# Accumulating transfers for two row-sum folds a batch, and the last half folded like the others

## The chip, the cores and the metric

One core of a Trainium2 chip runs the whole program. The metric is device time in microseconds (us); the kernel before takes 1115.96 us (median of three runs, 1114.64 to 1117.03).

## The reference

Pooled attention over 8 batches and 8 heads, followed by a top-1 mixture of experts. Shapes: q, k, v are 8 x 8 x 1152 x 64.

```python
q_pool = q.reshape(B, H, S // 2, 2, D).mean(axis=3)          # 576 queries
scores = scale * np.matmul(q_pool, k.transpose(0, 1, 3, 2))
attn = np.exp(scores - max(scores)); attn /= sum(attn) + 1e-09
x = np.matmul(attn, v)                                       # -> 4608 tokens of 512
logits = x @ w_gate; expert = argmax(logits); gate = softmax(logits)[expert]
out = gate * (np.maximum(x @ w1[expert], 0) @ w2[expert])
```

## The kernel before, in words

The attention comes first, the experts behind it. The attention is cut into 64 units: batch b (8), head pair hp (4 a batch), half (288 of the 576 queries). A unit is written here as (hp, half) of its batch. In a unit `scores` makes nine score products on TensorE (L640, each four matmuls on 64x64 quarters of the array, from 1,152 keys in nine chunks of 128), VectorE copies each one out of PSUM and takes its minimum (L644), the minima are spread over the partitions by a small product (L665), and ScalarE takes the exponentials in place, two chunks an instruction (L675). The tile `s` holds them: 128 partitions x 9 chunks x 2 heads x 288. `values` multiplies the exponentials by v (L779).

The softmax's divisor, the sum over 1,152 keys, is made in `chunk_sum`. It is the part that changes:

- Most units are folded on POOL into a tile `fold` of three chunks, by three adds: chunks 0 to 2 plus 3 to 5 (`fold<-s`), plus chunks 6 to 8 (`fold<-fold,s`, both 128 x 1728), and the third of the three onto the first (`fold<-fold`, 128 x 576). When both halves of a pair are folded, TensorE adds over the partitions with matmuls by a matrix of ones on 32-column tiles (`total`, L725): two groups of four.
- The last half of a batch, (3,1), has only the first add on POOL (L731); TensorE takes the other six chunks' worth itself (`whole`, L718): three groups of four beside the one of `total` for the other half of the pair.
- The last pair of the last batch is summed by TensorE alone.

There are three `fold` buffers and four `s` buffers. A fold buffer comes free when the pair's sum on TensorE has read it. POOL also adds neighbouring queries (`qp<-qn`, L529), issues six scatters a batch that enter the tokens into the experts' lists (L960), and later the experts' gathers. The loads of q, k and v are issued by SP.

The order of the work is written by a planner (`Flow.emit`, L135): every step has an engine, an assumed duration, a key (its rank), what it depends on and the buffers it holds; each engine takes the ready step with the lowest key, and the resulting order is then fixed for each engine. The constants `R_...` and `K_...` are added to the keys. TensorE's steps also carry the tiling they use (`COLS` for 32-column tiles, `QUADS` for quarters), and the planner prefers to stay in one.

Of the kernel before, what the change touches and what calls it, by code (L numbers as in the profile page):

```python
# [32 lines left out]
K_POOL = -28  # L33
# [4 lines left out]
K_SUM = 25  # L38
K_AV = 42
K_FREE = -25  # L40
R_Q = 18
R_K = 14
R_SCORE = -2
R_TAKE = -12
R_BIAS = -29
R_FOLD3 = 22
R_VALUE = 4
R_ADD = -17
R_LOGIT = -3
K_ROW = 33  # L50
K_ROUTE = 59
# [221 lines left out]
def kernel(  # L273
# [210 lines left out]
    def load_pair(o, f, key, b, hp):  # L484

        x = Pools()
        x.later, x.late = {}, hp
        opening = not o.exact and b == 0 and hp == 0
        if opening:
            return first_pair(o, f, key, x)  # L490

        kp = tile_of(o, "kp", [P, NQD * NC, BL], bufs=2, pool=o.ld)
        qn = tile_of(o, "qn", [P, NJ, NB, 2, BL], pool=o.ld)
        x.vn = vn = tile_of(o, "vn", [P, 2, NC, D], bufs=3, pool=o.rt)
        qp = tile_of(o, "qp", [P, NJ, NB, BL], pool=o.ld)
        x.kT = kT = tile_of(o, "kT", [P, NC * P], bufs=KT_BUFS, pool=o.kq)
        x.qT = qT = tile_of(o, "qT", [P, NQ], bufs=KT_BUFS, pool=o.kq)

        load = lambda out, src: nc.sync.dma_start(out=out, in_=src)
        rows = NQD * NC  # L500

        def quarters(t, src, n0=0, n1=rows):

            for h in range(2):
                for i in range(D // BL):
                    g = (h * D // BL + i) * BL
                    load(t[g:g + BL, n0:n1], src[h][:, i * BL:(i + 1) * BL].rearrange("(p n) d -> p n d", p=BL)[:, n0:n1])

        def k_part(n0, n1, ns, move, after=()):
            return f.carry("SP", ns, lambda: quarters(kp.t, heads(k, b, hp), n0, n1), key + K_LOAD, after, [kp], move)  # L510

        start = not o.exact and b == 0 and hp == 1

        def q_part(n0, n1, ns, move):
            return f.carry("SP", ns, lambda: quarters(qn.t.rearrange("p j b t d -> p (j b t) d"), heads(q, b, hp), n0, n1),
                    key + K_LOAD, (), [qn], move, 3000 if first and hp == 2 else 0)

        js = [slice(half * NJ // 2, (half + 1) * NJ // 2) for half in range(2)]
        first = not o.exact and b == 0
        paced = first and hp < 3  # L520
        move = 2600 if o.exact else 4400
        k0 = k_part(0, rows, 1900, move, done(not start and o.asked or None))
        cuts = [(0, rows // 2), (rows // 2, rows)] if start else [(0, rows)]
        q0 = [q_part(n0, n1, 1900 // len(cuts), move // len(cuts)) for n0, n1 in cuts]
        vb = heads(v, b, hp).rearrange("h (p b c) d -> b p h (c d)", b=NQD, c=NC)
        x.v = f.carry("SP", 1900, lambda: [load(vn.t[i * BL:(i + 1) * BL].rearrange("p h c d -> p h (c d)"), vb[i]) for i in range(NQD)],
                      key + K_V, done(q0[-1] and q0[-1][9][0]), [vn], 2600 if o.exact else 2200)
        parts = js if start else [slice(0, NJ)]
        q1 = [f.add("POOL", pool(NJ * QP // len(parts)), lambda j=j: nc.gpsimd.tensor_tensor(  # L529
            qp.t[:, j], qn.t[:, j, :, 0, :], qn.t[:, j, :, 1, :], ALU.add), key + K_POOL, done(got), [qn, qp])  # L530
            for j, got in zip(parts, q0)]
        q1 = [q1[0], q1[-1]]
        o.asked = q0[-1] and q0[-1][9][0]
        key += K_PIECE + (START if start else 0)
        x.k, x.q = {}, {}

        def turn_k(c0, n):
            nc.vector.transpose(kT.t.rearrange("p (c b i) -> p b c i", b=NQD, i=BL)[:, :, c0:c0 + n],
                                kp.t.rearrange("p (b c) d -> p b c d", b=NQD)[:, :, c0:c0 + n])

        def turn_q(half):
            nc.vector.transpose(qT.t.rearrange("p (j b i) -> p j b i", b=NB, i=BL)[:, js[half]], qp.t[:, js[half]])

        def turned(half):
            x.q[half] = done(f.add("DVE", turn_ns(HQ), lambda: turn_q(half), key + 7 * half + R_Q, done(q1[half], paced and o.pace or None), [qT, qp]))
            o.turned.extend(x.q[half])

        turned(0)
        for c0 in range(0, NC, TURN):
            n = min(TURN, NC - c0)  # L550
            e = f.add("DVE", turn_ns(n * P), lambda c0=c0, n=n: turn_k(c0, n), key + 2 + c0 / 2 + R_K, done(k0, paced and o.pace or None), [kT, kp])
            o.turned.extend(done(e))
            x.k.update((c, done(e)) for c in range(c0, c0 + n))
        turned(1)
        return x

# [64 lines left out]
    def scores(o, f, key, x, half, step=None):  # L621
# [8 lines left out]
        for c in range(NC):  # L630
            if half == 0 and c in x.later:
                x.later[c](done(m))
            pt = score_banks(o)

            def product(c=c, pt=pt):

                for i in range(2):
                    for h in range(2):
                        up, to = slice(h * D, (h + 1) * D), slice(i * D, (i + 1) * D)
                        nc.tensor.matmul(pt.t[to, h, :HQ], x.kT.t[up, c * P + i * D:c * P + (i + 1) * D], x.qT.t[up, cols],  # L640
                                         start=True, stop=True, tile_position=(up.start, to.start))

            def take(c=c, pt=pt):
                nc.vector.tensor_scalar(  # L644
                    s.t[:, c], pt.t[:, :, :HQ], -SCALE, None, op0=ALU.mult, op1=ALU.min, accum_out=mx.t[:, c:c + 1],
                )

            at = key + 20.0 * c / NC
            m = f.add("PE", 485, product, at + R_SCORE, done(*x.q[half], *x.k.get(c, ())), [pt, s, x.kT, x.qT], QUADS)
            o.turned.extend(done(m))  # L650
            if half == 1 and c == 3 - x.late:
                o.pace = m
            taken.append(f.add("DVE", dve(2 * HQ), take, at + R_TAKE, done(m), [pt, s]))
        if o.exact:
            for h in range(2):
                rowwise(o, s.t[:, :, h])
# [4 lines left out]
        def spread():  # L661
            for i in range(2):
                for j in range(2):
# [3 lines left out]

        m = f.add("DVE", 150, lambda: nc.vector.tensor_reduce(top.t, mx.t, axis=AX.X, op=ALU.min),
                  key + 20 + K_MAX, done(*taken))
        m = f.add("PE", 130, spread, key + 20 + K_TOP, done(m), [pb], QUADS)  # L670
        m = f.add("DVE", 290, lambda: nc.vector.tensor_reduce(bias.t, pb.t[:, :, :D], axis=AX.XY, op=ALU.min),  # L671
                  key + 20 + K_TOP + R_BIAS, done(m), [pb])

        def expo(c0, n):
            nc.scalar.activation(s.t[:, c0:c0 + n], s.t[:, c0:c0 + n], AF.Exp, bias=bias.t, scale=-1.0)  # L675
# [2 lines left out]
        for c0 in range(0, NC, step or NC):  # L678
            n = min(step or NC, NC - c0)
            e = f.add("ACT", act(2 * n * HQ) + 190, lambda c0=c0, n=n: expo(c0, n),  # L680
                      key + 20 + K_EXP + c0, done(m), [s])
            made += [e] * n
        return s, made

# [20 lines left out]
    def chunk_sum(o, f, key, s, ready, b, hp, half, sm, last):  # L705
# [1 line left out]

        key += K_SUM
        by_units = not o.exact and b == B - 1 and hp >= NHP - LAST
        on_pe = by_units or not o.exact and hp == NHP - 1 and half == 1  # L710
        if half == 0 or by_units:
            o.pair, ps = None, None

        def whole(ps, begin, chunks):
            for i, chunk in enumerate(chunks):
                for h in range(2):
                    to = slice(64 * (i % 2) + 32 * h, 64 * (i % 2) + 32 * h + 32)
                    nc.tensor.matmul(ps.t[to, 0, :HQ], ones4[:, hp, half, :], chunk[:, h], start=begin and i < 2,  # L718
                                     stop=i + 2 >= len(chunks), tile_position=(0, to.start))

        def total(ps, u, half, begin):
            for i in range(2):
# [10 lines left out]
        elif not on_pe:  # L733
            u = tile_of(o, "fold", [P, 3, 2, HQ], bufs=FOLD_BUFS, pool=o.rt)
            add = lambda to, a, b: nc.gpsimd.tensor_tensor(to, a, b, ALU.add)  # L735
            p = f.add("POOL", pool(6 * HQ), lambda: add(u.t, s.t[:, 0:3], s.t[:, 3:6]), key, every(ready[:6]), [s, u])
            p = f.add("POOL", pool(6 * HQ), lambda: add(u.t, u.t, s.t[:, 6:9]), key, done(p, *every(ready[6:])), [s, u])
            p = f.add("POOL", pool(2 * HQ), lambda: add(u.t[:, 0], u.t[:, 0], u.t[:, 2]), key + R_FOLD3, done(p), [u])
            if half == 0:
                o.pair = (u, p)  # L740
                u.left += 1
# [3 lines left out]
        if o.pair:  # L745
            v, q = o.pair
            v.left -= 1
            parts.append(lambda: total(ps, v, 0, True))
            needs, holds, ns = done(q), [ps, v], 485
        begin = not parts  # L750
        if half_way:
            parts.append(lambda: whole(ps, begin, [*(u.t[:, c] for c in range(3)), *(s.t[:, c] for c in range(6, NC))]))
# [4 lines left out]
        else:  # L757
            parts.append(lambda: total(ps, u, 1, begin))
            needs, holds, ns = [*needs, *done(p)], [*holds, u], ns + 485
        p = f.add("PE", ns, lambda: [part() for part in parts], key + 15 - 5 * on_pe, needs, holds, COLS)  # L760
        if not last:
            return [f.add("ACT", act(HQ) - 44, lambda: nc.scalar.copy(sm.t, ps.t[:, 0, :HQ]), key + 15, done(p), [ps, sm])]
        return [f.add("DVE", dve(HQ), lambda: nc.vector.tensor_tensor(sm.t, sm.t, ps.t[:, 0, :HQ], ALU.add),
# [2 lines left out]
    def values(o, f, key, x, s, ready, hp, half, xT):  # L766
# [4 lines left out]
        for c in range(NC):  # L771
# [7 lines left out]
                        mark.made = nc.tensor.matmul(pa.t[cs, i, :HQ], x.vn.t[up, h, c, :], s.t[up, c, h],  # L779
                                                     start=c == 0, stop=c == NC - 1, tile_position=(up.start, cs.start))  # L780

            p = f.add("PE", 485, product, key + 20.0 * c / NC + R_VALUE, done(p, x.v, ready[c]), [pa, x.vn, s], QUADS)
            mark.step = p
            o.marks.append(mark)
        a = f.add("ACT", act(HQ) - 44, lambda: nc.scalar.copy(xT.t[:, hp, to], pa.t[:, 0, :HQ]), key + 20 + K_FREE, done(p), [pa, xT])
# [25 lines left out]
        return f.add("DVE", 600, inverse, key, done(p), [ps, rec])  # L811

    def attend(o, f, key, b, hp, xT, sm, summed):
        x = load_pair(o, f, key, b, hp)
        outs = []
        end = not o.exact and hp == NHP - 1 and b == B - 1
# [9 lines left out]
    def routing(o, f, key, b, xT, rec, ready, hold=()):  # L826
# [15 lines left out]

        if b is not None:
            f.add("DVE", 150, lambda: nc.vector.tensor_reduce(flg[:, b:b + 1], recf(), axis=AX.XY, op=ALU.max),
                  at, ready, [rec])
        pl = pt = pr = value_banks(o) if b == B - 1 else score_banks(o)

        aside = lambda at, n: pt.t[:QP, 1, at:at + n]
# [711 lines left out]
```

## Time and profile before

| | us |
|---|---|
| median of 3 runs | 1115.96 |
| profiled execution, its own time | 1113.62 |
| its span, first to last instruction | 1111.7 |
| TensorE (PE) busy in the span | 1100.8 |
| POOL busy in the span | 854.2 |
| granted TensorE clock, mean share | 0.999 |

The attention takes about the first 650 us, the experts the rest. One batch of the attention repeats every 80.07 us. PE, PEld, DVE, ACT, POOL and SP are TensorE's matmuls, its weight loads, VectorE, ScalarE, GpSimd and SyncE. An fp32 matmul stands in the trace as two records, so a group of four matmuls is eight records.

### The profile page before, as it was taken

The numbers are of one execution on the slowest core, as the hardware profiler recorded it, in microseconds if no ns is written. First come the engines' busy times: TensorE is split into PE (matmuls) and PEld (weight loads), VectorE is DVE, ScalarE is ACT, GpSimd is POOL, SyncE is SP. The second block draws the span as 40 slices with busy tenths as digits, with TensorE's granted clock in tenths as the row PEclk, the third lists the DMA queues.
The fourth block names the chain that finished last, engine by engine and source line by source line (L and its number), as shares of the span: only waits on it lengthen the run. The fifth ranks groups of instructions, "written<-read, shape, count | busy, mean of one in ns | idle before, by whom it ended". The sixth has DMA issues, their size and how long they took to land.

```text
span 1111.7 us, 32995 instructions
## 1 busy us (share of the span) xinstructions
PE 1100.8 (99%) x13317; PEld 793.8 (71%) x13317; DVE 875.5 (79%) x2244; ACT 624.2 (56%) x835; POOL 854.2 (77%) x488
## 2 busy tenths in 40 slices
PE   9999999999999999999999999999999999999997
PEld 5555556565655565665665568999888989899896
DVE  7988988989989989989999959755555556677761
ACT  4656666566565666557655564444444444555561
POOL 3999999999999999999999943766666655555511
PEclk9999999999999999999999999999999999999999
DMA  9976747738648558558545069865555566677640
GB/s 159 167 120 111 128 76 123 129 66 125 115 73 139 97 85 141 94 89 146 81 84 107 3 227 212 244 180 176 176 169 167 184 195 191 194 248 252 224 159 30
DMA packets 387502, 158.06 MB, mean 142 GB/s; under 512 B 302694, under 2 KB 357762, under 8 KB 387342
## 3 DMA queue, kind: packets, MB, share of 16 engines
q1 hardware_dynamic: 376718, 134.91, 55.7%
q0 software_dynamic: 10464, 20.78, 5.8%
q8 instruction: 106, 1.74, 0.7%
q14 instruction: 54, 0.44, 0.2%
q10 hardware_dynamic: 160, 0.20, 0.1%
HBM read 135.02 MB, written 22.07 MB: 141 GB/s over the span
## 4 chain that ended last, share of the span: by engine, by line
PE 87%; issue 7%; POOL 4%; DVE 1%; DMA 1%; POOLq 0%; ACT 0%
PE st L640 24%; PE pa L779 24%; PE ph L1363 16%; PE py L1393 16%; PE st L725 3%; POOL fold L735 2%; PE st L718 1%; DVE s L644 1%; POOL xr L1092 1%; PE st L856 1%; PE st L665 1%; POOL out_dram L1402 1%; POOL xq L1092 1%; PE st L801 0%; DMA xr<-x_runs,ix 0%
## 5 line engine op out<-in xcount | busy, mean ns | idle before, releaser
L675 ACT ACTIVATE s<-s,bias 128x1152 f32<-128x1152 f32 (+1 forms) x320 | 346.7, 1149 | 172.5 <-DVE bias L671 172.4
L644 DVE TENSOR_SCALAR_CACHE_REDUCE s<-st 128x576 f32<-128x576 f32 x576 | 416.1, 746 | 30.3 <-PE st L640 28.1
L640 PE MATMUL st<-qT,kT 64*64 64x288 f32 x4608 | 363.6, 406 | 1.5 <-DVE s L644 0.9
L779 PE MATMUL pa<-s,vn 64*64 64x288 f32 x4608 | 358.5, 403 | 0.3 <-DVE xT L786 0.3
L640 PEld LDWEIGHTS st<-qT,kT 64*64 64x64 f32 x4608 | 167.4, 133 | 115.3 <-DVE s L644 22.4
L779 PEld LDWEIGHTS pa<-s,vn 64*64 64x64 f32 x4608 | 172.2, 133 | 98.4 <-DVE xT L786 3.5
L735 POOL TENSOR_TENSOR fold<-s 128x1728 f32<-128x1728 f32 x55 | 212.9, 3870 | 4.6 <-ACT s L675 4.4
L735 POOL TENSOR_TENSOR fold<-fold,s 128x1728 f32<-128x1728 f32 x55 | 213.4, 3879 | 0.5
L1363 PE MATMUL ph<-xh,w1h 128*128 128x248 f32 (+4 forms) x512 | 155.8, 304 | 0.6 <-DVE hl L1373 0.6
L1363 PE MATMUL ph<-xl,w1h 128*128 128x248 f32 (+4 forms) x512 | 154.6, 302 | 0.0
L1363 PE MATMUL ph<-xh,w1l 128*128 128x248 f32 (+4 forms) x512 | 154.6, 302 | 0.0
L1235 DVE TENSOR_TENSOR w2l<-raw,w2h 128x1024 fp32r<-128x1024 f32 x64 | 78.3, 1223 | 85.0 <-ACT w2h L1320 81.3
L1092 POOL DMA_INDIRECT xr<-x_runs,ix x76 | 96.8, 1274 | 51.8 <-issue 23.9
L1393 PE MATMUL py<-w2h,hh 128*128 128x512 f32 x328 | 128.1, 391 | 0.0
L1393 PE MATMUL py<-w2l,hh 128*128 128x512 f32 x328 | 127.8, 390 | 0.0
L1393 PE MATMUL py<-w2h,hl 128*128 128x512 f32 x328 | 127.8, 390 | 0.0
L1402 POOL DMA_INDIRECT out_dram<-y,rec x41 | 44.0, 1073 | 90.0 <-ACT y L1410 73.1
L1371 ACT ACTIVATE hh<-ph 128x372 fp32r<-128x372 f32 (+4 forms) x100 | 49.3, 493 | 106.5 <-PE ph L1363 106.4
L1363 PEld LDWEIGHTS ph<-xh,w1h 128*128 128x128 f32 x512 | 96.4, 188 | 3.4 <-DVE hl L1373 1.5
L1363 PEld LDWEIGHTS ph<-xl,w1h 128*128 128x128 f32 x512 | 96.5, 188 | 0.8
L1363 PEld LDWEIGHTS ph<-xh,w1l 128*128 128x128 f32 x512 | 96.5, 188 | 0.0
L1373 DVE SCALAR_TENSOR_TENSOR hl<-ph,hh 128x372 fp32r<-128x372 f32 (+4 forms) x100 | 55.6, 556 | 48.6 <-ACT hh L1371 48.5
(230 smaller groups left out, 1339.0 us busy)
## 6 DMA issues: line engine op xcount, KB each, us to landing
raw<-in_moe_w_dram SPq DMA_DIRECT2D x128, 512.0 KB
kp<-in_k_dram SPq DMA_DIRECT2D x124, 144.0 KB
vn<-in_v_dram SPq DMA_DIRECT2D x124, 144.0 KB
qn<-in_q_dram SPq DMA_DIRECT2D x120, 144.0 KB
x_runs<-row SPq DMA_DIRECT2D x96, 99.0 KB
xr<-x_runs,ix POOLq DMA_INDIRECT x76, 4.7
x_runs<-empty SPq DMA_DIRECT2D x4, 297.0 KB
xq<-x_runs,ix POOLq DMA_INDIRECT x52, 2.9
```

The lines of the kernel that those rows point to most:

```text
L640: nc.tensor.matmul(pt.t[to, h, :HQ], x.kT.t[up, c * P + i * D:c * P + (i + 1) * D], x.qT.t[up, cols], start=True, stop=True, tile_position ...
L644: nc.vector.tensor_scalar(s.t[:, c], pt.t[:, :, :HQ], -SCALE, None, op0=ALU.mult, op1=ALU.min, accum_out=mx.t[:, c:c + 1],)
L675: nc.scalar.activation(s.t[:, c0:c0 + n], s.t[:, c0:c0 + n], AF.Exp, bias=bias.t, scale=-1.0)
L735: add = lambda to, a, b: nc.gpsimd.tensor_tensor(to, a, b, ALU.add)
L779: mark.made = nc.tensor.matmul(pa.t[cs, i, :HQ], x.vn.t[up, h, c, :], s.t[up, c, h], start=c == 0, stop=c == NC - 1, tile_position=(up.sta ...
L1092: ins = nc.gpsimd.indirect_dma_start(out=x.xr[i // NQD].t[:, i % NQD, :], out_offset=None, in_=xg, in_offset=bass.IndirectOffsetOnAxis(ap= ...
L1235: (nc.gpsimd if eng == "POOL" else nc.vector).tensor_tensor(lo, raw, hi.bitcast(F32), ALU.subtract)
L1363: mark.made = nc.tensor.matmul(view()[:, i, :], a[:, c, fp], b[:, c, :n], start=c == 0 and k == 0, stop=c == NDC - 1 and k == 2)
L1371: a = f.add("ACT", act(nb * n) - 44, lambda home=home, apart=apart: nc.scalar.activation(home(0), apart(), AF.Relu), at - 20, done(p), [ph ...
L1373: d = f.add("DVE", dve(nb * n), lambda home=home, apart=apart: nc.vector.scalar_tensor_tensor(home(1), apart(), 0.0, home(0).bitcast(F32), ...
L1393: mark.made = nc.tensor.matmul(py.t, blocks(a)[:, c * x.nr + r], b[:, c % 2, :], start=c == 0 and k == 0, stop=c == NFC - 1 and k == 2)
L1402: ins = nc.gpsimd.indirect_dma_start(out=out, out_offset=bass.IndirectOffsetOnAxis(ap=x.re.t.bitcast(I32)[:, r, 0:1], axis=0), in_=y.t, in ...
```

## The change

From the second batch on (b > 0, `o.later`), the steps get ranks of their own: each `R_...` constant becomes a pair, the second of which is for later batches, and five new ones are added (the short list below shows three). For b = 1 to 6 the second add of units (0,0) and (2,0) is no longer a POOL add but a transfer that POOL issues and that adds chunks 6 to 8 into the fold tile (`dma_start` with `accum_op`). And only in batch 0 does the last half still go to TensorE (`on_pe`); in batches 1 to 6 it is folded by three POOL adds like any other. The variable `one` is always false, so what hangs on it does nothing.

```diff
-R_Q = 18
-R_FOLD3 = 22
+R_Q = 18, 37
+R_FOLD3 = 22, 40
+R_SUM = 0, -1
+R_EXP = 0, 38
+R_POOL = 0, -21
...
-        on_pe = by_units or not o.exact and hp == NHP - 1 and half == 1
+        on_pe = by_units or not o.exact and b == 0 and hp == NHP - 1 and half == 1
...
+        one = not o.exact and (False)
...
-            p = f.add("POOL", pool(6 * HQ), lambda: add(u.t, u.t, s.t[:, 6:9]), key, done(p, *every(ready[6:])), [s, u])
-            p = f.add("POOL", pool(2 * HQ), lambda: add(u.t[:, 0], u.t[:, 0], u.t[:, 2]), key + R_FOLD3, done(p), [u])
+            if not o.exact and (half == 0 and 0 < b < B - 1 and hp % 2 == 0):
+                p = f.add("POOL", 1100, lambda: nc.gpsimd.dma_start(out=u.t, in_=s.t[:, 6:9], accum_op=ALU.add), key, done(p, *every(ready[6:])), [s, u])
+                p = f.add("DMA", 4700, lambda: None, key, done(p), [s, u], late=800)
+            else:
+                p = f.add("POOL", pool(6 * HQ), lambda: add(u.t, u.t, s.t[:, 6:9]), key, done(p, *every(ready[6:])), [s, u])
+            p = f.add("POOL", pool(2 * HQ), lambda: add(u.t[:, 0], u.t[:, 0], u.t[:, 2]), key + R_FOLD3[o.later], done(p), [u])
...
-        p = f.add("PE", ns, lambda: [part() for part in parts], key + 15 - 5 * on_pe, needs, holds, COLS)
+        p = f.add("PE", ns, lambda: [part() for part in parts], key + 15 - 5 * on_pe + R_SUM[o.later], needs, holds, COLS)
...
     def attend(o, f, key, b, hp, xT, sm, summed):
+        o.later = int(not o.exact and b > 0)
```

On TensorE before, around the sum of the fourth batch's last pair (`fold_4723` is unit (3,0), `fold_4858` unit (3,1), `pa` and `st` the products with v and the scores):

```order
L640 MATMUL st_5040<-qT_4870,kT_4721 64x288 x4
L779 MATMUL pa_4947<-s_4568,vn_4222 64x288 x4
L725 MATMUL st_5057<-fold_4723,ones_73 32x288 x4
L718 MATMUL st_5057<-fold_4858,ones_73 32x288 x6
L718 MATMUL st_5057<-s_4568,ones_73 32x288 x6
L640 MATMUL st_5083<-qT_4870,kT_4721 64x288 x4
```

The same place on TensorE in the changed kernel (`fold_4710` is (3,0), `fold_4837` is (3,1)):

```order
L645 MATMUL st_5047<-qT_4718,kT_4731 64x288 x4
L645 MATMUL st_5052<-qT_4718,kT_4731 64x288 x4
L732 MATMUL st_5060<-fold_4710,ones_73 32x288 x4
L732 MATMUL st_5060<-fold_4837,ones_73 32x288 x4
L645 MATMUL st_5079<-qT_4718,kT_4731 64x288 x4
```

Sixteen matmuls of the sum have become eight, and the sum now needs the finished fold of (3,1). On POOL before, from the same batch's last half to the next batch's first units (`fold_4932` is the next batch's (0,0), `fold_5089` its (0,1)):

```order
L735 TENSOR_TENSOR fold_4723<-fold_4723,s_4433 128x1728
L529 TENSOR_TENSOR qp_4840<-qn_4331 128x576
L731 TENSOR_TENSOR fold_4858<-s_4568 128x1728
L735 TENSOR_TENSOR fold_4723<-fold_4723 128x576
L735 TENSOR_TENSOR fold_4932<-s_4690 128x1728
L529 TENSOR_TENSOR qp_4990<-qn_4860 128x576
L735 TENSOR_TENSOR fold_4932<-fold_4932,s_4690 128x1728
L735 TENSOR_TENSOR fold_4932<-fold_4932 128x576
L735 TENSOR_TENSOR fold_5089<-s_4814 128x1728
```

And on POOL in the changed kernel (`fold_4976` is the next batch's (0,0), `fold_5087` its (0,1)):

```order
L742 TENSOR_TENSOR fold_4837<-s_4558 128x1728
L534 TENSOR_TENSOR qp_4882<-qn_4569 128x576
L742 TENSOR_TENSOR fold_4837<-fold_4837,s_4558 128x1728
L742 TENSOR_TENSOR fold_4710<-fold_4710 128x576
L742 TENSOR_TENSOR fold_4976<-s_4685 128x1728
L742 TENSOR_TENSOR fold_4837<-fold_4837 128x576
L745 DMA fold_4976<-s_4685 128x1728
L534 TENSOR_TENSOR qp_5069<-qn_4901 128x576
L742 TENSOR_TENSOR fold_5087<-s_4822 128x1728
L742 TENSOR_TENSOR fold_5087<-fold_5087,s_4822 128x1728
L742 TENSOR_TENSOR fold_4976<-fold_4976 128x576
```

The last half has three adds, the last of them behind the next batch's first one; between the issue of the transfer and the add that needs it stand one `qp` and two full adds. At the other transfer, that of unit (2,0), there stand two full adds, two short ones and three scatters.

## Rows read from the trace of the kernel before

**Rows 1.** The page, busy time of each engine in the span
```profile
PE 1100.8 (99%) x13317; PEld 793.8 (71%) x13317; DVE 875.5 (79%) x2244; ACT 624.2 (56%) x835; POOL 854.2 (77%) x488
```

**Rows 2.** Busy time of each engine in 80 us, one batch of the attention
```profile
core 0: us, PE busy (x) PEld busy (x) DVE busy (x) ACT busy (x) POOL busy (x), PEclk, DMA share, GB/s
412.00:492.00 80.00, 80.00 (x1332) 48.36 (x1328) 73.52 (x221) 49.71 (x66) 78.38 (x33) 1.00 0.63 106
```

**Rows 3.** Timeline of PE: start us, us, instruction; a last pair's sum
```profile
424.38 0.69 PE L725 MATMUL st<-fold,ones 128*32 128x288 f32 x8
424.89 0.90 PE L718 MATMUL st<-fold,ones 128*32 128x288 f32 x10
...
425.63 0.90 PE L718 MATMUL st<-s,ones 128*32 128x288 f32 x10
426.46 0.71 PE L640 MATMUL st<-qT,kT 64*64 64x288 f32 x8
```

**Rows 4.** Timeline of PE, the other sums until the next last pair's
```profile
445.94 1.18 PE L725 MATMUL st<-fold,ones 128*32 128x288 f32 x16
447.05 0.72 PE L640 MATMUL st<-qT,kT 64*64 64x288 f32 x8
...
467.50 1.18 PE L725 MATMUL st<-fold,ones 128*32 128x288 f32 x16
...
486.46 1.18 PE L725 MATMUL st<-fold,ones 128*32 128x288 f32 x16
...
504.45 0.69 PE L725 MATMUL st<-fold,ones 128*32 128x288 f32 x8
```

**Rows 5.** Timeline of POOL, a list scatter between two adds; the last half's add
```profile
384.42 3.87 POOL L735 TENSOR_TENSOR fold<-fold,s 128x1728 f32<-128x1728 f32 x1
388.45 0.92 POOL L960 DMA_INDIRECT lists<-re,di  x1 [0.17 <-issue]
389.39 3.89 POOL L735 TENSOR_TENSOR fold<-s 128x1728 f32<-128x1728 f32 x1
...
411.12 3.90 POOL L731 TENSOR_TENSOR fold<-s 128x1728 f32<-128x1728 f32 x1
```

**Rows 6.** Timeline of POOL, its one wait in a batch; the next last half
```profile
446.80 3.86 POOL L735 TENSOR_TENSOR fold<-s 128x1728 f32<-128x1728 f32 x1 [0.35 <-ACT s L675]
...
484.64 1.41 POOL L735 TENSOR_TENSOR fold<-fold 128x576 f32<-128x576 f32 x1
486.01 3.85 POOL L735 TENSOR_TENSOR fold<-fold,s 128x1728 f32<-128x1728 f32 x1
489.83 1.40 POOL L529 TENSOR_TENSOR qp<-qn 128x576 f32<-128x576 f32 x1
491.19 3.88 POOL L731 TENSOR_TENSOR fold<-s 128x1728 f32<-128x1728 f32 x1
```

**Rows 7.** By tile: POOL's DMA issues, ns min/median/max; from issue to landing
```profile
L960 POOL DMA_INDIRECT lists<-re,di x48: 915/922/1710, 130.7 to 684.6; - x48
L1051 POOL DMA_DIRECT2D rec<-lists x13: 669/787/812, 694.9 to 929.9; - x13
DMA to landing us min/median/max: 3.4/5.1/6.1
...
L1092 POOL DMA_INDIRECT xr<-x_runs,ix x76: 991/1060/2012, 704.2 to 1046.6; - x76
DMA to landing us min/median/max: 3.1/4.7/7.2
```

**Rows 8.** Busy time and DMA share (second last column) in two stretches of the batch
```profile
424.00:434.00 10.00, 10.00 (x166) 5.78 (x162) 8.58 (x25) 5.99 (x13) 9.92 (x5) 1.00 1.07 159
...
462.00:478.00 16.00, 16.00 (x271) 9.63 (x266) 13.66 (x39) 11.22 (x12) 15.44 (x7) 1.00 0.47 76
```

More of the change, by code (lines that the diff above doesn't have):

```diff
@@ L40 @@
 K_FREE = -25
-R_Q = 18
[L42 to L45, printed above, removed]
-R_FOLD3 = 22
-R_VALUE = 4
-R_ADD = -17
+R_Q = 18, 37
+R_K = 14, 37
+R_SCORE = -2, -3
+R_TAKE = -12, 14
+R_BIAS = -29, 31
+R_FOLD3 = 22, 40
+R_VALUE = 4, 3
+R_ADD = -17
+R_FLAG = 0, 21
+R_SUM = 0, -1
+R_EXP = 0, 38
+R_SPREAD = 0, 3
+R_POOL = 0, -21
 R_LOGIT = -3
@@ L529, in load_pair @@
         q1 = [f.add("POOL", pool(NJ * QP // len(parts)), lambda j=j: nc.gpsimd.tensor_tensor(
-            qp.t[:, j], qn.t[:, j, :, 0, :], qn.t[:, j, :, 1, :], ALU.add), key + K_POOL, done(got), [qn, qp])
+            qp.t[:, j], qn.t[:, j, :, 0, :], qn.t[:, j, :, 1, :], ALU.add), key + K_POOL + R_POOL[o.later], done(got), [qn, qp])
             for j, got in zip(parts, q0)]
@@ L544, in turned @@
         def turned(half):
-            x.q[half] = done(f.add("DVE", turn_ns(HQ), lambda: turn_q(half), key + 7 * half + R_Q, done(q1[half], paced and o.pace or None), [qT, qp]))
+            x.q[half] = done(f.add("DVE", turn_ns(HQ), lambda: turn_q(half), key + 7 * half + R_Q[o.later], done(q1[half], paced and o.pace or None), [qT, qp]))
             o.turned.extend(x.q[half])
@@ L550, in load_pair @@
             n = min(TURN, NC - c0)
-            e = f.add("DVE", turn_ns(n * P), lambda c0=c0, n=n: turn_k(c0, n), key + 2 + c0 / 2 + R_K, done(k0, paced and o.pace or None), [kT, kp])
+            e = f.add("DVE", turn_ns(n * P), lambda c0=c0, n=n: turn_k(c0, n), key + 2 + c0 / 2 + R_K[o.later], done(k0, paced and o.pace or None), [kT, kp])
             o.turned.extend(done(e))
@@ L648, in scores @@
             at = key + 20.0 * c / NC
-            m = f.add("PE", 485, product, at + R_SCORE, done(*x.q[half], *x.k.get(c, ())), [pt, s, x.kT, x.qT], QUADS)
+            m = f.add("PE", 485, product, at + R_SCORE[o.later], done(*x.q[half], *x.k.get(c, ())), [pt, s, x.kT, x.qT], QUADS)
             o.turned.extend(done(m))
@@ L652, in scores @@
                 o.pace = m
-            taken.append(f.add("DVE", dve(2 * HQ), take, at + R_TAKE, done(m), [pt, s]))
+            taken.append(f.add("DVE", dve(2 * HQ), take, at + R_TAKE[o.later], done(m), [pt, s]))
         if o.exact:
@@ L669, in scores @@
                   key + 20 + K_MAX, done(*taken))
-        m = f.add("PE", 130, spread, key + 20 + K_TOP, done(m), [pb], QUADS)
+        m = f.add("PE", 130, spread, key + 20 + K_TOP + R_SPREAD[o.later], done(m), [pb], QUADS)
         m = f.add("DVE", 290, lambda: nc.vector.tensor_reduce(bias.t, pb.t[:, :, :D], axis=AX.XY, op=ALU.min),
-                  key + 20 + K_TOP + R_BIAS, done(m), [pb])
+                  key + 20 + K_TOP + R_BIAS[o.later], done(m), [pb])
         def expo(c0, n):
@@ L680, in scores @@
             e = f.add("ACT", act(2 * n * HQ) + 190, lambda c0=c0, n=n: expo(c0, n),
-                      key + 20 + K_EXP + c0, done(m), [s])
+                      key + 20 + K_EXP + c0 + R_EXP[o.later], done(m), [s])
             made += [e] * n
@@ L736, in chunk_sum @@
             p = f.add("POOL", pool(6 * HQ), lambda: add(u.t, s.t[:, 0:3], s.t[:, 3:6]), key, every(ready[:6]), [s, u])
-            p = f.add("POOL", pool(6 * HQ), lambda: add(u.t, u.t, s.t[:, 6:9]), key, done(p, *every(ready[6:])), [s, u])
-            p = f.add("POOL", pool(2 * HQ), lambda: add(u.t[:, 0], u.t[:, 0], u.t[:, 2]), key + R_FOLD3, done(p), [u])
+            if not o.exact and (half == 0 and 0 < b < B - 1 and hp % 2 == 0):
[4 more added lines that the diff above has]
+            p = f.add("POOL", pool(2 * HQ), lambda: add(u.t[:, 0], u.t[:, 0], u.t[:, 2]), key + R_FOLD3[o.later], done(p), [u])
+            if one:
+                p = f.add("POOL", pool(2 * HQ), lambda: add(u.t[:, 0], u.t[:, 0], u.t[:, 1]), key, done(p), [u])
             if half == 0:
@@ L748, in chunk_sum @@
             parts.append(lambda: total(ps, v, 0, True))
-            needs, holds, ns = done(q), [ps, v], 485
+            needs, holds, ns = done(q), [ps, v], 0 if one else 485
         begin = not parts
@@ L780, in product @@
                                                      start=c == 0, stop=c == NC - 1, tile_position=(up.start, cs.start))
-            p = f.add("PE", 485, product, key + 20.0 * c / NC + R_VALUE, done(p, x.v, ready[c]), [pa, x.vn, s], QUADS)
+            p = f.add("PE", 485, product, key + 20.0 * c / NC + R_VALUE[o.later], done(p, x.v, ready[c]), [pa, x.vn, s], QUADS)
             mark.step = p
@@ L844, in routing @@
             f.add("DVE", 150, lambda: nc.vector.tensor_reduce(flg[:, b:b + 1], recf(), axis=AX.XY, op=ALU.max),
-                  at, ready, [rec])
+                  at + R_FLAG[o.later], ready, [rec])
         pl = pt = pr = value_banks(o) if b == B - 1 else score_banks(o)
```

## The prediction

> **What bounds the kernel now.** Busy time first, then the batch, then each sum. Over the span PE is busy 1100.8 of 1111.7 us [rows 1], and in one batch of the attention 80.00 of 80.00 us, VectorE 73.52, POOL 78.38 [rows 2]. So a matmul that goes shortens the batch, as long as no other engine is nearly as full; POOL is. The timelines give both periods. The last pair's sum comes at 424.38 and again at 504.45 us: PE's period is 80.07 us [rows 3, 4]. The last half's add on POOL comes at 411.12 and at 491.19: 80.07 us too [rows 5, 6]. POOL stands still in it for want of work only once, 0.35 us at 446.80 [rows 6]. The row names ScalarE, but the add starts 0.86 us after the sum at 445.94 [rows 4], about when its matmuls have read the fold buffer that the add takes. POOL's own work is thus 80.07 - 0.35 = 79.72 us a batch, gaps before scatters included. PE leads by a third of a microsecond.
>
> **TensorE's part.** The last pair's sum takes 424.38 to 426.46, 2.08 us; a pair with both halves folded takes 445.94 to 447.05, 1.11 us [rows 3, 4]. Both include going to the 32-column tiles and back. The change turns the one into the other: 0.97 us, in the sums of batches 1 to 6, since batch 0 is kept and the last batch never had this form. 6 x 0.97 = 5.8 us, all of it on the engine that has no idle time. The number of times PE changes its tiling stays: still four sums and one set of logits a batch. PE's period becomes 80.07 - 0.97 = 79.10 us if nobody makes it wait.
>
> **POOL's part.** A full add takes 3.82 us from its start to the next one's (486.01 to 489.83), a short one 1.37 (484.64 to 486.01) [rows 6]. Each batch loses two full adds (-7.64), and the last half gains a full and a short one (+5.19): -2.45 us. It gains two issues of transfers. What one costs on POOL the trace doesn't show; issues of other kinds bound it. The direct copies over 120 or so partitions take 0.79 us, the scatter of 96 rows 0.92, the gather of 128 rows 1.06 (medians) [rows 7]. The gap goes on top: an add and a scatter together take 389.39 - 384.42 = 4.97 us [rows 5], less 3.82 makes 1.15 for the scatter, 0.23 over its own length. So an issue costs 1.02 to 1.29. The direct copy is the nearest in form, the gather in its number of rows; I take the value between, 1.15. POOL's work is then 79.72 - 2.45 + 2.30 = 79.57 us a batch (79.31 to 79.85), against PE's 79.10. POOL has become the longer of the two, by 0.47 (0.21 to 0.75), so part of TensorE's gain can't be had.
>
> **How much lag PE forgives.** In the changed order PE makes 72 score and value products between the sum of pair 1 and that of pair 3, before 70. Before, this took 504.45 - 467.50 = 36.95 us [rows 4]; two more products at 0.485 (a sum's group is 0.97 / 2, a product is also eight records) make 37.92. POOL in this stretch must begin the first add of (2,1) when the sum of pair 1 has freed a buffer, 0.86 us after its start, and get to the end of (3,1)'s short add: by its order seven full adds, five short ones (`qp` counted) and two scatters, 7 x 3.82 + 5 x 1.37 + 2 x 1.15 = 35.9. The handing over to PE takes 0.4 (an add that starts at 484.64 and lasts 1.41 is followed by its sum at 486.46 [rows 4, 6]). 0.86 + 35.9 + 0.4 = 37.1, which leaves 0.8 us. So POOL can be some 0.7 late once before PE stands; then every further microsecond of POOL is one of PE.
>
> **The sum.** 5.8 saved, less 6 x 0.47 - 0.7 = 2.1 given back to POOL: -3.7 us. With the issue at 1.02 it is -5.3, at 1.29 -2.0. The profiled execution (1113.62 us, span 1111.7) would come to 1109.9; the median of the runs is 2.3 above that execution, so 1115.96 - 3.7 = 1112.3 us.
>
> **What I cost at nothing.** The transfer itself moves 128 x 1728 x 4 B = 0.88 MB and is waited for by the short add of its unit, on POOL, in order. At (0,0) there stand behind the issue a `qp` and two full adds, 1.37 + 2 x 3.82 = 9.0 us; at (2,0) two full and two short adds and three scatters, 13.8. Transfers that POOL issued landed after 5.1 and 4.7 us in the median, 7.2 at most [rows 7], but were smaller. The one at (0,0) is issued soon after the last half's fold, near 424 to 430, and there the DMA engines are full: share 1.07, 159 GB/s; the one at (2,0) falls near 462 to 478, where the share is 0.47 [rows 8]. If the transfer were given all of those 159 GB/s it would need 5.6 us, at half of them 11.1, plus a fixed part of a few microseconds. My range for its landing is 5 to 13 us; I take 8, since most rows are near 5, so that 9.0 just covers it. What it costs without that cover is the second rival. The Trainium skill (DMA: Bandwidth & Descriptors, Anatomy of one DMA) fits a transfer that GpSimd issues with 2.0 us plus its bytes at 436 GB/s, here an estimate of 4.0 us, which would leave the sum as it is; the full stretch of the trace speaks against using it unloaded.
>
> The new ranks move VectorE's transposes and ScalarE's exponentials by a few places. VectorE has 6.5 us a batch to spare [rows 2], and the `qp` adds now stand over 20 us ahead of the products that need them; against it `qp` must wait for VectorE to have read the last one, which the order puts just before it. I price this at 0, between -1 and +1.5 us over the six batches. The experts' part (from the first product on) stands in the same order on PE as before: 0.
>
> **Rivals.**
> 1. PE alone decides: POOL's issue costs 1.0 or less with its gap, or there is more room for lag than I found. Then the whole 5.8 come: 1110.2. For it: before, POOL ran equally full without holding up PE. Against it: the issue would have to be as short as the shortest row.
> 2. The transfer lands late, the one that ends slower. Place: the short add of (0,0), behind a transfer that shares full DMA engines with the loads. Every microsecond beyond 9.0 lengthens POOL's batch, with POOL already the longer. From 9.6 on, 6 x 0.6 = 3.6 eat the gain; at 11.1 + 2 it is 6 x 4.1 = 24.6, thus 1112.3 + 24.6 = 1136.9; at 10.5 it is 9.0: 1121.3. For it: share 1.07, and an accumulation must read two streams for one written, which no row shows. Against it: packets of a second queue need not wait for all of the first, and 7.2 was the slowest landing of the rows. The Trainium skill (Trainium Kernel Development and Optimization, Key Constraints) says that DMAs from SP, ACT and POOL run on the same 16 engines and interleave; by it the transfer would get a share of the full engines and not all, which is this rival.
> 3. The issue is dear: 1.71 us, the longest scatter [rows 7], with its gap 1.94. POOL's batch is 81.15, 2.05 over PE's: 5.8 - (12.3 - 0.7) = -5.8, slower: 1121.8. Against it: that scatter is one of 48, and its median is 0.92.
> 4. No change: issue at 1.4 with gap, or the transfer half a microsecond late: 1114 to 1117.
>
> **Chances.** Forecast 0.46, rival 1 0.16, rival 4 0.20, rival 2 0.12, rival 3 0.06. A change of under 0.2% (2.2 us) can't be told from none. The forecast's end at -2.0 falls into that, so a part of 0.04 of it counts as no change: faster 0.58, within 0.2% 0.24, slower 0.18. The range: 1109.0 (rival 1, and 1.2 from the new ranks) to 1118.0, which takes in rival 4 and the beginning of 2 and 3 and leaves about 2 in 10 out. The likeliest case's own is 1110.4 to 1114.0.
>
> **What would show it.** The last pair's sum as 16 records of L732 in 1.1 us, and the period from one to the next: 79.6 by the forecast, 79.1 by rival 1, over 80.1 by rivals 2 and 3. The issue's duration on POOL (0.8 to 1.1). Idle time of POOL before the short add that follows a transfer: none, or rival 2. PE's weight loads waiting for POOL's fold at pair 3's sum, about half a microsecond a batch. POOL without any wait for PE in the later batches. Wrong would be a POOL that waits each batch for PE while PE is slower than 79.1, or a PE that waits for VectorE.

## The result, and the profile after

| | kernel before | changed kernel |
|---|---|---|
| median of 11 runs | 1115.35 us (1113.86 to 1117.53) | 1136.28 us (1119.15 to 1150.82) |
| profiled execution, its span | 1113.62, 1111.7 us | 1129.23, 1127.7 us |
| granted clock, mean | 0.999 | 0.991 |

The forecast was 1112.3 us. The changed kernel is slower, and its eleven executions spread over 32 us, those before over 4. The ratio of the comparison, 1.0085 with a 95% interval of 1.0057 to 1.0112, counts only executions within 1.5% of the fastest; six of the eleven lie above that, so the medians' ratio is 1.0188.

In the page of the changed kernel, the busy line answers to [rows 1], and the queue that POOL's transfers use (q0) now has 12 x 0.88 MB more, 31.39 in place of 20.78:

```profile
PE 1101.8 (98%) x13221; PEld 792.8 (70%) x13221; DVE 874.9 (78%) x2244; ACT 624.9 (55%) x835; POOL 854.3 (76%) x500
...
q0 software_dynamic: 12192, 31.39, 10.9%
```

PE is busy a microsecond longer with 96 records fewer: busy shares hide what happened. From one last pair's sum to the next, [rows 3, 4], the periods of batches 1 to 6 are 91.51, 79.44, 79.66, 79.73, 82.27 and 86.55 us. Three came as forecast (79.6); in the other three the excess over 79.6 is 11.9, 2.7 and 7.0 us. The 11.9 and the 7.0 are followed below. In the batch with 2.7 no `qp` add stands until its last 1.1 us; there PE stops in the middle of pair 2's sum, for nothing that the profile shows ("issue"), and what held it is open:

```profile
496.30 1.17 PE L732 MATMUL st<-fold,ones 128*32 128x288 f32 x13 [1.26 <-issue]
```

In a quiet stretch PE's timeline shows the sum in its new form, 16 records of L732, and then with a small wait:

```profile
353.26 1.40 PE L732 MATMUL st<-fold,ones 128*32 128x288 f32 x16
354.59 0.45 PE L645 MATMUL st<-qT,kT 64*64 64x288 f32 x1
...
432.99 0.69 PE L732 MATMUL st<-fold,ones 128*32 128x288 f32 x8
433.90 0.69 PE L732 MATMUL st<-fold,ones 128*32 128x288 f32 x8 [0.22 <-POOL fold L742]
```

Now the worst batch, 102.65 to 194.16. POOL's timeline around the transfer at (2,0), in place of [rows 5, 6]:

```profile
141.17 1.04 POOL L745 DMA_DIRECT2D fold<-s  x1
141.82 1.84 POOL L742 TENSOR_TENSOR fold<-fold 128x576 f32<-128x576 f32 x1
143.84 0.99 POOL L974 DMA_INDIRECT lists<-re,di  x1 [0.18 <-issue]
154.77 1.41 POOL L534 TENSOR_TENSOR qp<-qn 128x576 f32<-128x576 f32 x1 [9.95 <-PE pa L792]
156.14 3.87 POOL L742 TENSOR_TENSOR fold<-s 128x1728 f32<-128x1728 f32 x1
```

The issue takes 1.04 us, as bounded. But the `qp` add stands 9.95 us, with all of POOL's folds behind it. The row names a product of TensorE, but TensorE had been at work all the while (busy 10.00 of 10.00 us in 144 to 154). The add needs two things: that VectorE has read the old content of `qp`, and that the next q has been loaded. The first was done early:

```profile
144.83 0.47 DVE L547 STREAM_TRANSPOSE qT<-qp 128x288 f32<-128x288 f32 x1
```

So it waits for the load. SyncE's queue in the same stretch:

```profile
137.53 11.61 SPq L504 DMA_DIRECT2D qn<-in_q_dram  x4
149.23 5.80 SPq L504 DMA_DIRECT2D kp<-in_k_dram  x4
```

and for comparison, two q loads of the kernel before, the second with its add, which did not stand:

```profile
515.19 3.53 SPq L499 DMA_DIRECT2D qn<-in_q_dram  x4
...
571.37 4.97 SPq L499 DMA_DIRECT2D qn<-in_q_dram  x4
...
580.35 1.41 POOL L529 TENSOR_TENSOR qp<-qn 128x576 f32<-128x576 f32 x1
```

The four pieces of the q load took 11.61 us to issue; in batches 1 to 6 of the kernel before it was 3.2 to 7.3. The add follows the end of the issue by 5.6 us; before, the closest add started 4.0 behind it (580.35, the row above). The DMA queues between 143 and 148 us (packets, MB, share of the 16 engines) show who was ahead of them:

```profile
q0 software_dynamic: 133, 0.79, 84.5%
q1 hardware_dynamic: 628, 0.08, 12.6%
```

q0 carries POOL's transfer, q1 SyncE's loads. The transfer is 128 pieces of 6912 B, eight for each of 16 DMA engines, and a piece takes 536 to 626 ns on average over a transfer (twelve transfers): 4.3 to 5.0 us of an engine's time. The Trainium skill (DMA: Bandwidth & Descriptors, Queues, rings and completion order) says that an engine empties a whole packet of one queue, about 9 to 17 descriptors, before it turns to the next. That q1 is all but silent while q0 has eight pieces an engine agrees with that; the trace doesn't tell the engines apart.

What followed at PE, and the same stretch as windows (the last three numbers of a line are the granted clock, the DMA share and GB/s):

```profile
163.29 1.15 PE L645 MATMUL st<-qT,kT 64*64 64x288 f32 x16
167.59 0.69 PE L732 MATMUL st<-fold,ones 128*32 128x288 f32 x8 [3.16 <-POOL fold L742]
172.72 1.19 PE L732 MATMUL st<-fold,ones 128*32 128x288 f32 x8 [4.43 <-POOL fold L742]
173.83 1.24 PE L645 MATMUL st<-qT,kT 64*64 64x288 f32 x8
```

```profile
162.00:166.00 4.00, 2.44 (x42) 1.22 (x32) 4.00 (x14) 1.86 (x3) 3.83 (x2) 1.00 0.14 22
166.00:170.00 4.00, 0.69 (x8) 0.16 (x8) 0.04 (x2) 0.00 (x0) 3.98 (x3) 0.83 0.63 98
170.00:174.00 4.00, 1.28 (x12) 0.37 (x16) 0.03 (x1) 0.00 (x0) 4.00 (x3) 0.50 0.80 116
174.00:178.00 4.00, 4.00 (x44) 2.14 (x48) 1.48 (x4) 1.22 (x2) 4.00 (x2) 0.50 0.70 141
178.00:182.00 4.00, 4.00 (x64) 2.30 (x60) 2.30 (x6) 4.00 (x5) 4.00 (x3) 0.89 0.00 0
```

PE stands 3.16 and 4.43 us for the fold. During the second standing the granted clock goes to 0.50 (1.2 GHz), and between 174 and 178 PE does 44 records where 4 us at full clock hold 66 [rows 2]. That is 7.6 us of standing; the clock stays low for 10.2 us, 6.2 of them with PE at work at half speed, which by estimate costs 3.1 of the remaining 4.3. Batch 6 repeats it: `qp` waits 7.51 us at 563.83, PE 1.10 and 4.43, and the clock is 0.50 for 6.8 us.

Whether a batch is hit is decided within about 2 us. At (2,0) of batch 1 the q load's issue ended 8.0 us after the transfer's issue began (wait 9.95), in batch 6 0.8 after (7.51); in batches 2, 3, 4 and 5 it ended 1.4, 1.4, 1.7 and 3.2 before, and the waits are 1.9, 0, 0.6 and 0. The runs below repeat it: in runs 3, 4, 5 and 7 eight more q loads ended their issue 0.5 to 2.5 us after that of a transfer began, and their adds stood 5.0 to 9.1 us. In run 1, where the transfer is thin, one ended 0.3 us after, and its add stood 0.7; in run 2, where the load has more slack, one ended 1.5 after, and its add didn't stand. That this is the spread from run to run is likely (the fastest execution has a mean clock of 0.998, the three slowest 0.982 to 0.986), but not shown: only one of the eleven has a trace.

### The profile page after: what moved, and what is told of

It is laid out like the page before. It is cut to its first block, busy times and chain, and to the rows that moved or that the text cites. A ratio compares the mean times of both kernels' runs of the same rounds, so it can differ in the third digit from the quotient of the medians.

```text
span 1127.7 us, 32814 instructions
## 1 busy us (share of the span) xinstructions
PE 1101.8 (98%) x13221; PEld 792.8 (70%) x13221; DVE 874.9 (78%) x2244; ACT 624.9 (55%) x835; POOL 854.3 (76%) x500
## 3 DMA queue, kind: packets, MB, share of 16 engines
q0 software_dynamic: 12192, 31.39, 10.9%
## 4 chain that ended last, share of the span: by engine, by line
PE 74%; POOL 8%; issue 6%; DMA 5%; SPq 3%; DVE 2%; ACT 1%; POOLq 0%; DVEq 0%; ACTq 0%
PE pa L792 18%; PE st L645 18%; PE py L1407 17%; PE ph L1377 16%; POOL fold L742 6%; SPq L504 3%; DMA qn<-in_q_dram 3%; PE st L732 2%; DMA kp<-in_k_dram 1%; DVE s L649 1%; PE st L870 1%; PE st L723 1%; ACT s L680 0%; PE st L670 0%; POOL out_dram L1416 0%
## 5 line engine op out<-in xcount | busy, mean ns | idle before, releaser
L742 POOL TENSOR_TENSOR fold<-s 128x1728 f32<-128x1728 f32 x61 | 238.4, 3908 | 2.1 <-ACT s L680 2.0
L742 POOL TENSOR_TENSOR fold<-fold,s 128x1728 f32<-128x1728 f32 x49 | 191.0, 3897 | 0.6
L1249 DVE TENSOR_TENSOR w2l<-raw,w2h 128x1024 fp32r<-128x1024 f32 x64 | 78.2, 1223 | 84.5 <-ACT w2h L1334 80.8
L1106 POOL DMA_INDIRECT xq<-x_runs,ix x52 | 60.2, 1157 | 45.9 <-PE py L1407 21.6
```

Source lines behind the costliest of these rows:

```text
L1106: ins = nc.gpsimd.indirect_dma_start(out=x.xr[i // NQD].t[:, i % NQD, :], out_offset=None, in_=xg, in_offset=bass.IndirectOffsetOnAxis(ap= ...
L1249: (nc.gpsimd if eng == "POOL" else nc.vector).tensor_tensor(lo, raw, hi.bitcast(F32), ALU.subtract)
```

## The experiments

Theory A: the transfer holds the DMA engines, the q load behind it is late, and since there is one q buffer the load can't be asked for earlier. The rivals: B, the new places of the `qp` adds; C, the order of SyncE's queue; D, the transfers by themselves. E and F stand with the runs that test them. The kernel before took 1115.8 us on the chip of the first four runs and 1118.8 to 1118.9 on the two chips of the others, so gains are told as ratios.

**1. Thin transfers.** Same instructions and order, hardly any data.

```
- ... dma_start(out=u.t, in_=s.t[:, 6:9], accum_op=ALU.add) ...
+ ... dma_start(out=u.t[:, 0, 0, :16], in_=s.t[:, 6, 0, :16], accum_op=ALU.add) ...
```

> The changed kernel with its twelve transfers cut to 16 of 1728 numbers a partition (what they leave out isn't added, so the row sums of these units are wrong); the order on every engine is that of the changed kernel, and POOL still issues twelve transfers. Theory A (a full transfer keeps all 16 DMA engines for about 5 us, the q load behind it comes late, and POOL stands in order before its qp add): no qp add waits over 1 us, the period of a batch is 79.5 to 79.8 us in all batches, 1111 to 1113 us, runs within 3 us of each other. Rival B (the new ranks put qp too early for the loads, whatever the transfers do): qp still waits, 1119 us or more, spread over 10 us.

Only the attention can be compared, since the row sums lack a part and the experts' part then has other work (1339.3 us in all): periods 80.69, 79.21, 79.33, 79.20, 79.24, 79.21, one `qp` wait of 0.7 us. Ranks, issues and folds are as in the changed kernel; without the bytes the loss is gone. POOL's waits from 110 to 600 us, where the changed kernel had 9.9 + 7.5 us of `qp` and more:

```profile
POOL qp L534 <- DVE qT L547: 0.7, 1, 0.7
```

**2. Two q buffers, known to the planner** (`qn=1` becomes `qn=2`).

> The changed kernel with a second buffer for the q load (qn=2 in the planner's list), so that each q load is issued a pair earlier; POOL's order is unchanged and the transfers are whole. Theory A: the loads are delayed as before but have 15 to 20 us more, qp never waits for them, period 79.5 to 79.8 us, 1111 to 1114 us. Rival C (it is the transfer itself that comes late, or its issue that is dear): nothing changes, 1119 to 1151 us. Rival B: as theory A here, told apart by the cut transfers.

1114.95 us, ratio 0.9995 (0.9984 to 1.0005), against 1111 to 1114 expected. Periods 80.69 and then 79.20 to 79.32 with whole transfers, as A says; but the first batch ends at 108.93 us, not 102.65. There the planner now lets q loads go ahead of k and v, and the gain is used up. The expectation is wrong in one point: with the second buffer the planner wrote another order for every engine, POOL too. The buffer by itself is run 5.

**3. Transfers alone, in the kernel before** (old ranks, last half still summed by PE; the fold of (0,0) and (2,0) becomes a transfer).

> The kernel before with the twelve transfers in place of folds and nothing else: old ranks, the last half of a batch still summed on TensorE. TensorE keeps its period of 80.07 us, and POOL has about 5 us a batch to spare (79.72 - 7.64 + 2.3 = 74.4). Theory A: the q loads are late here as well where a qp add stands right behind a transfer, POOL's spare time takes up most of it: 1115 to 1122 us, qp waits of 2 to 10 us visible. If the transfers alone cost nothing: 1115 to 1117 us and no qp wait.

1134.99 us, ratio 1.0168 (1.0130 to 1.0206), more than expected: `qp` waits of 41 us in all in the profiled execution, eight of them over 1 us. They are of two kinds, for the q load and for VectorE, which must have read the pair before's `qp` (110 to 600 us):

```profile
POOL qp L529 <- DMA qn<-in_q_dram: 26.3, 5, 9.1
POOL qp L529 <- DVE qT L542: 15.1, 5, 5.4
```

Neither the new ranks nor the last half are needed for the loss.

**4. Plain copies of the same bytes** (the transfer without `accum_op`).

> The changed kernel with the transfers as plain copies of the same size from the same queue (the fold tile is overwritten instead of added to, so the sums are wrong). If the adding makes a piece of 6912 bytes take 600 ns on a DMA engine, the copy takes about 280 (4096 bytes took 167) and holds the engines 2.3 us instead of 5: qp waits of 0 to 4 us, 1111 to 1118 us. If it is the size of the pieces and the queue and not the adding, the pieces take 600 ns here too and the time is 1119 us or more.

A copied piece takes 282 to 397 ns on average over a transfer, an accumulated one 536 to 626: adding nearly doubles the hold. But the copies still held up loads in two batches (84.78 and 86.91 us, waits 5.2 and 7.3, over the 4 expected); the others ran at 79.21 to 79.43. So it is not the adding alone: a plain transfer of this size does it too. (1408 us in all isn't comparable.)

**5. Two q buffers in turn, every instruction at its old place.**

```
  qn = tile_of(o, "qn", [P, NJ, NB, 2, BL], pool=o.ld,
+              name="qn" if o.exact else f"qn{hp % 2}")
```

> The changed kernel with two q-load buffers used in turn; every instruction stays at its place in every queue (in the run before with a second buffer the first batch's loads were reordered and lost 6 us). Theory A (a transfer holds up the q load behind it, and the single buffer leaves the load no slack): the waits of the qp adds fall from 22 us to under 5 us, the batches' periods go to 79.2-79.5 us, the first batch keeps its 102.6 us, and the total is 1109.5-1112 us. Rival C (the sync engine's order holds the q load up anyway, behind loads of k and v that wait for their own buffers): waits of over 10 us stay, 1120-1136 us. Rival D (the transfers cost by themselves, whatever the loads do): periods near 80, 1115-1118 us.

1113.26 us, ratio 0.9947 (0.9927 to 0.9966): 5.6 us faster than before. The order on every engine is that of the changed kernel, so the buffer alone does it, and A is right on the size. The profiled execution is the slowest of its seven (1123.69) and shows C too: its periods are 81.59, 79.80, 79.21, 86.14, 85.36 and 79.50, and `qp` waits of 14 us in all stand where A expected under 5. Two of them are long; SyncE's queue and POOL's timeline at the second:

```profile
459.45 9.09 SPq L504 DMA_DIRECT2D qn<-in_q_dram  x4
```

```profile
467.23 1.03 POOL L745 DMA_DIRECT2D fold<-s  x1
...
476.97 1.42 POOL L534 TENSOR_TENSOR qp<-qn 128x576 f32<-128x576 f32 x1 [6.11 <-DVE s L649]
```

The load stands behind v and k in SyncE's queue and can still end just after a transfer's issue, here 1.3 us.

**6. The same two buffers in the kernel before.**

> The kernel before with the same two q-load buffers and nothing else. Theory A: no q load is late there, so nothing changes: 1115-1116.5 us, periods 80.1 us. Rival E (the second buffer is itself worth the gain): 1109-1113 us.

1119.67 us, ratio 1.0014 (0.9998 to 1.0031): the buffer alone is worth nothing.

**7. Transfers alone with two buffers** (run 3 with the edit of run 5).

> The kernel before with the twelve accumulating transfers and two q-load buffers, old ranks, the last half still summed by TensorE; with one buffer this was 1135.0 us. Theory A: the 19 us of the transfers go, since the load may now come 10 us late: 1114-1117 us, qp waits under 5 us in all against 41. Rival C or D: at least half of the loss stays, 1124 us or more.

Ratio 1.0034 (1.0009 to 1.0058), 1123.55 us: four fifths of the loss of run 3 goes, not all of it. The profiled execution (1131.36 us) still has 29 us of `qp` waits, where A expected under 5; but those for a load have become 9.4, and 19.3 are for VectorE (110 to 600 us):

```profile
POOL qp L529 <- DVE qT L542: 19.3, 7, 4.9
POOL qp L529 <- DMA qn<-in_q_dram: 9.4, 2, 7.1
```

The late load of 7.1 us makes its batch 87.06; the others take 80.66 to 81.38, against 80.49 to 81.15 in run 6 on the same chip. So the waits for VectorE cost little: POOL has the time here.

**8. Old rank of the `qp` adds** (`R_POOL = 0, 0`), one buffer.

> The changed kernel with one buffer, but the rank of the qp adds from the second batch on as in the kernel before (0 in place of -21). Theory A: the buffer is as scarce at either place, a transfer still makes the load up to 10 us late; 1119-1140 us with waits of the qp adds over 10 us in all. Rival F (it is the early place of the qp adds in GpSimd's queue that turns the late load into a wait): waits under 5 us, 1109-1113 us.

1134.5 us, ratio 1.0136 (1.0115 to 1.0158), and neither theory: the `qp` waits fall from 22 to one of 6.0 us, near what F says, yet the batches without one take 81.8 to 82.9, the last 85.2. PE's weight loads wait for VectorE instead; from 290 to 580 us, first here and then in run 11:

```profile
PEld st L645 <- DVE s L649: 14.6, 33, 1.1
PEld pa L792 <- DVE xT L799: 6.8, 22, 1.3
```

```profile
PEld st L646 <- DVE s L650: 11.1, 31, 0.5
...
PEld pa L793 <- DVE xT L800: 0.3, 2, 0.2
```

That is 10 us more in some 3.5 batches, about what they are longer by. So the early place has its share in the loss: at the old one the add leaves a late load enough time. But with the other ranks new, the old place costs more than it saves.

**9. Ranks alone**, no transfers, last half on PE.

> The kernel before with the new ranks from the second batch on and nothing else: no transfers, the last half still summed by TensorE, one q buffer. Theory A (the transfers alone make loads late): no qp wait over 1 us, periods 80.0-80.6 us, ratio 0.998-1.003. Rival B (the new places of the qp adds are late or early by themselves): qp waits of over 5 us in all, or a ratio of 1.006 or more.

Ratio 1.0043 (1.0029 to 1.0057), between the two. No `qp` wait over 1 us, but periods of 82.09 and then 80.79 to 81.48: by the ratio these ranks cost 4.8 us, 0.8 a batch, where the work they were set for isn't there. By themselves they make no load late.

**10. POOL's own folds in place of the transfers.**

> The changed kernel with GpSimd's own folds in place of all twelve transfers; the last half is folded like the others and the ranks are new. GpSimd then has 79.2 us of work in a batch of the changed kernel plus two folds of 3.8 us less two issues of 1.0 us, 84.8 us: theory A expects periods of 84.5-85.5 us with GpSimd never waiting, and 1140-1150 us in all. If it came out under 1125 us the transfers would not be needed for the change's saving.

1143.29 us, ratio 1.0227 (1.0195 to 1.0259); the last four periods are 84.6 to 85.5. The transfers are needed: POOL has no room for the last half without them.

**11. The best version**: two buffers that the planner uses from batch 1 on.

```
+ more = [hold_of("qn", None)] if not o.exact and b == 0 else []
...
- ... key + K_LOAD, (), [qn], move, ...
+ ... key + K_LOAD, (), [qn, *more], move, ...
...
- ... done(got), [qn, qp])
+ ... done(got), [qn, qp, *more])
...
- f = Flow(dict(st=S_BUFS, s=UNITS, qn=1, ...
+ f = Flow(dict(st=S_BUFS, s=UNITS, qn=2, ...
```

> The changed kernel with two q-load buffers that the planner of the order knows of from the second batch on, while a q load of the first batch takes both: the first batch keeps the order of the changed kernel, the loads behind it go ahead as in the run that reordered everything. Theory A: first batch's last sum at 102.6-103.1 us, periods of 79.2-79.3 us, no wait of a qp add over 2 us in the batches, so 6 times 0.85 us under the kernel before and steadier than the run whose order was kept: 1115.8 less 5 to 7 us on a chip like that of the first runs, a ratio of 0.9935 to 0.9955. Rival C (late loads come back elsewhere once the first batch is faster): ratio of 0.998 or more.

1113.95 us (1111.95 to 1116.23) against 1118.79, ratio 0.9958 (0.9945 to 0.9972): 4.8 us faster than before, just under the 5 to 7 that A expected, and steadier than run 5. The periods are 81.34, 79.21, 79.37, 79.50, 79.55 and 79.53, where 79.2 to 79.3 was expected. A batch, and the sum at its end:

```profile
345.00:424.50 79.50, 79.50 (x1316) 47.38 (x1312) 73.17 (x221) 49.79 (x65) 78.33 (x36) 1.00 0.76 129
```

```profile
424.50 1.18 PE L733 MATMUL st<-fold,ones 128*32 128x288 f32 x16
425.61 0.72 PE L646 MATMUL st<-qT,kT 64*64 64x288 f32 x8
```

No `qp` wait stands after 150 us. The first batch's sum is at 105.08, 2.5 us late, which takes a part of the gain; against run 5 the two intervals overlap.

## Why the prediction was wrong

- **TensorE's part** held in its mechanism: the last pair's sum is 16 records in 1.11 us (run 11). Without late loads most of PE's periods are 79.20 to 79.21 (runs 1, 2) where 79.10 was forecast, a saving of 0.87 a batch and not 0.97.
- **POOL's part** held. The issue takes 0.94 to 1.15 us; the next add starts 0.65 us after it but lasts longer, so that from 353.87 to 360.16 two adds and the issue cost 6.29 us, 1.10 more than the adds (forecast 1.15). In run 2 POOL takes 79.48 us a batch, 317.93 us for four, without a wait of its own over 0.2 us (forecast 79.57), while PE's sums of the last pairs run at 79.21, 316.83 for four:

```profile
214.94 1.40 POOL L534 TENSOR_TENSOR qp<-qn 128x576 f32<-128x576 f32 x1
...
532.87 1.41 POOL L534 TENSOR_TENSOR qp<-qn 128x576 f32<-128x576 f32 x1
```

```profile
189.62 1.18 PE L732 MATMUL st<-fold,ones 128*32 128x288 f32 x16
...
506.45 1.29 PE L732 MATMUL st<-fold,ones 128*32 128x288 f32 x16
```

So POOL is the longer of the two, by 0.27 and not 0.47, and PE forgives more of it than the 0.7 us forecast: about 1.1 us in these four batches without a longer period, until the last of these sums takes 1.29 us in place of 1.18. That the quiet batches of the changed kernel (79.44 to 79.73) meet the forecast 79.57 is in part luck: without late loads they go at 79.2, as rival 1 has it.
- **The transfer's landing** was forecast at 8 us and its last piece ended 6.4 to 9.1 us after the issue. No short add of the changed kernel waited for it. Rival 2 thus named a late transfer, but the wrong waiter: at (0,0), its place, nothing stood over 1.2 us. That its 1136.9 us is near the measured median is chance; it belongs to a landing after 13.1 us.
- **The step that failed** is "What I cost at nothing". It priced the transfer only by who waits for its result, and the moved `qp` adds at 0, -1 to +1.5, on the ground that they stand over 20 us ahead of the products. That margin is the products'; the margin that broke is the one before the add, from the first piece of the q load's issue to `qp`. At the add behind (2,0) the kernel before has 37 us of it in batches 2 to 6; the changed order leaves 14.8, and 9.2 in batch 1 (run 1, where the transfers hold nothing). With the transfers, the adds of the two hit batches start 17.2 and 18.1 us after it. The prediction gave the bytes of the transfer no effect on the loads behind them, and the moved add no price for its data. In the profiled execution the two batches lose 18.9 us; that PE's standing halves its clock for 10.2 and 6.8 us was in no term either.
- The Trainium skill's rule cited in rival 2 (Trainium Kernel Development and Optimization, Key Constraints), that the DMAs of SP, ACT and POOL share the engines and interleave, was read as taking turns by small shares. In 143 to 148 us the transfer had 84.5% of the engines' time and the loads 12.6%, a turn of nearly the whole transfer.
- A slip: the low end of the likeliest case, 1110.4, should be 1110.7 by its own sum (1115.96 - 5.3).
- **Is it shown?** Without the bytes, the waits go (run 1); with the bytes and a second buffer the forecast gain is there (runs 5, 11); the buffer alone is worth nothing in the kernel before (run 6); the transfers make the loss without the new ranks too (run 3), though in an order of their own. Runs 1 and 5 keep the changed order on every engine. Open are the late load that stays in run 7, the cost of the ranks in run 9, the stop of 1.26 us, and the 0.3 us by which run 11's batches exceed 79.2. A part of that may be the chip's: on another than the first, batches of the kernel before with two buffers take 80.49 and more (run 6) against 80.07, and in both runs the difference lies between the sums of pairs 0 and 1.

## What to carry to other kernels

Price a DMA by what it does to the transfers behind it, not only by who waits for its result: write down for each load how long it takes from issue to first use in the trace, and ask which of them has no buffer to spare. Do the same for an add that a new order moves: its margin to its data, not only to its readers. A second buffer for the tight load turned a loss of 1 to 2% into a gain of 0.4 to 0.5%. Where executions of one kernel spread by 3%, look for two events whose order is decided by a microsecond or two.

## What the runs showed of the hardware

- An accumulating transfer within the core's memory takes 536 to 626 ns for a piece of 6912 B on average over a transfer, a copy of the same pieces 282 to 397. While one ran, SyncE's loads came nearly to a stop: 12.6% of the engines' time in 143 to 148 us against 84.5%.
- TensorE's granted clock went from 1.00 to 0.50 in a stretch in which it stood 3.16 and 4.43 us with eight matmul records between, and again in one with 1.10 and 4.43, both times during the second standing (0.83 in 166 to 170, 0.50 in 170 to 174). PE worked from 172.72 on, and the clock was 0.50 in 174 to 178, 0.89 in 178 to 182 and 1.00 in 182 to 186.
